# Float64 weights decoded in pieces of 1024 columns into tiles laid out by chunk, with scratch tiles given up one by one

## Chip, cores and metric

The kernel runs on one core of a Trainium2 chip. The metric is the device time of one execution in microseconds (us). Three runs are compared by their median.

## What is computed

Attention over 4 batches and 8 heads, 576 tokens, head size 64, with a mask by blocks of 64; then a gated layer with weights of 512 x 1536; then a layer of 8 experts of which each token takes one.

```python
scores = scale * np.matmul(q, k.transpose(0, 1, 3, 2))
scores = np.where(block_i >= block_j, scores, -1000000000.0)
attn = softmax(scores)                       # written out in the reference
x = np.matmul(attn, v)                       # (4, 8, 576, 64) -> (2304, 512)
gate = 1.0 / (1.0 + np.exp(-(x @ w_gate)))   # w_gate, w_val: 512 x 1536
x = gate * (x @ w_val) @ w_out               # w_out: 1536 x 512
idx = np.argmax(x @ r_gate, axis=1)          # 8 experts
out = prob[idx] * (np.maximum(x @ w1[idx], 0.0) @ w2[idx])
```

`w_gate`, `w_val` and `w_out` reach the kernel as float64, seen as pairs of 32-bit words. The kernel makes of each weight a high and a low float32r part, so that matmuls with both keep float32 accuracy.

## The kernel before

**Stages.** The *quick stage* is attention of batch 0: four pairs of heads (0 to 3), each with five tiles of queries (t = 0 to 4). Then the *gated stage* runs over nine units of 256 tokens (`u`), in each over 12 chunks `f` of 128 columns of the gated layer: `m_gate` and `m_val` (24 matmuls into `gv`), `m_act` (tanh on ScalarE, `th` on VectorE, `g` high on ScalarE, `g` low on VectorE) and, one chunk later, `m_out` (matmuls into `acc`). Attention of batches 1 to 3 is threaded into it. The expert stage ends the kernel. TensorE, VectorE, ScalarE, GpSimd and SyncE are called PE, DVE, ACT, POOL and SP, as in the profile.

**Order.** Every engine runs its instructions in the order in which the program is written. In the quick stage, strings set it: step `i` of `quick` works on tile `a = i + 2` (S scores, M maximum, E exponential, r and c reciprocal of the sum, N scaling), on tile `i + 1` (T, U transposes) and on tile `i` (V product with `v`, X its split into `x`). K and Q transpose the next pair's `k` and `q` and copy them to `kn` and `qn`. A `d` gives the weight decode one step.

```python
Q2 = "SVTMXdUEdrcN"
Q3 = "dSVMXKdTUErcdN"
...
    if i >= 0 and items[i][1] == 0 and 0 < items[i][0]:
        load(items[i][0] + 1)
```

So the loads of the next pair but one (`load`: two heads of `k`, the last tokens of `k` and of `q`, then `q`, then `v`, all on SP's DMA queue) are written at the end of the step with i at t = 0 of a pair; the K that uses them stands in the next step (Q3).

**Decode.** A piece is loaded by one DMA into a ring of raw tiles. On DVE it takes a shift with mask (L545), a mask-and-or (L549), an integer add (L553, shown as CUSTOM or ISA) and the subtraction that gives the low part (L562); on ACT a conversion (L544) and the copy that gives the high part (L560). The raw tile is free after the mask-and-or. The generator `weights` interleaves these steps for three pieces. Chunks 0 to 7 are 24 pieces of 512 columns (`g`, `v`, `o` of each chunk), decoded in scratch cut from six `spare` tiles; a loop drains them all ahead of the gated stage. Then all six spare tiles are given up together, and chunks 8 to 11 follow as 24 pieces of 256 columns in small scratch (`wtmp`, `wt`), during unit 0.

Of the kernel before, what the change touches and what calls it, by code (L numbers as in the profile page):

```python
# [18 lines left out]
P = 128  # L19
# [5 lines left out]
def attn_moe_moe_kernel(  # L25
# [107 lines left out]
    def wtile(name):  # L133
        return wp.tile([P, 2048], F32R, tag="w", name=name, bufs=18)

    FG = KF // 3
    wmat = {}

    spare = [wtile(f"spare{i}") for i in range(6)]

    def wgroup(g):
        for nm in ("g", "v", "o"):
            for part in ("h", "l"):
                wmat[nm, part, g] = wtile(f"w{nm}{part}{g}")

    wgroup(0)
    wgroup(1)

    def w_in(nm, part, kk, f):
        o = kk * 512 + (f % FG) * P  # L150
        return wmat[nm, part, f // FG][:, o:o + P]

    def w_o(part, f):
        o = (f % FG) * 512
        return wmat["o", part, f // FG][:, o:o + 512]


    pairs = [(b, hp) for b in range(B) for hp in range(NP)]
# [241 lines left out]
    def attention():  # L400
# [1 line left out]
        load(0, "kq")  # L402
        wfirst[0](FIRST)
        load(0, "v")
        wfirst[0](4)
        prep(0, "k")
        prep(0, "q")
        load(1)
# [86 lines left out]

    wide = w_gate.dtype == mybir.dt.int64
    wn = 2 if wide else 1
    pieces = []
    upto = []
    for f in range(KF):  # L500
        fo = (f % FG) * P
        n = KD if f < 2 * FG else KD // 2
        for nm, src in (("g", w_gate), ("v", w_val)):
            for a in range(0, KD, n):
                def cut(part, nm=nm, f=f, a=a, n=n, fo=fo):
                    t = wmat[nm, part, f // FG].rearrange("p (k c) -> p k c", k=KD)
                    return t[:, a:a + n, fo:fo + P]
                pieces.append((cut, src, a * P, f * P, n, P))
        for a in range(0, DM, n * P):
            def cut(part, f=f, a=a, n=n):  # L510
                t = wmat["o", part, f // FG].rearrange("p (k c) -> p k c", k=FG)
                return t[:, f % FG:f % FG + 1, a:a + n * P]
            pieces.append((cut, w_out, f * P, a, 1, n * P))
        upto.append(len(pieces))
    wq = []
    wload = [0]
    wdone = [0]
    wlim = [upto[2 * FG - 1]]
    words = spare[0].bitcast(I32).rearrange("p (b c) -> p b c", c=512)
    wb = [words[:, i, :] for i in range(3)]  # L520
    wres = [words[:, 3, :], spare[1].bitcast(I32)[:, 0:512]]
    wring = []

    def w_load(n):
        while wload[0] < min(n, wlim[0]):
            cut, src, r0, c0, nk, ncol = pieces[wload[0]]
            raw_ = wring[wload[0] % len(wring)]
            raw_ = raw_.rearrange("p (k c w) -> p k c w", k=nk, w=wn)
            words = src.bitcast(I32)[r0:r0 + nk * P, c0 * wn:(c0 + ncol) * wn]
            nc.sync.dma_start(  # L530
                out=raw_.rearrange("p k c w -> p k (c w)"), in_=words.rearrange("(k p) c -> p k c", p=P)
            )
            wq.append((cut, raw_))
            wload[0] += 1

    def w_round(n, stage):

        raw_ = wq[n][1]
        nk = raw_.shape[1]
        w0, w1 = raw_[:, :, :, 0], raw_[:, :, :, 1]  # L540
        b = wb[n % len(wb)].rearrange("p (k c) -> p k c", k=nk)
        r = wres[n % 2].rearrange("p (k c) -> p k c", k=nk)
# [12 lines left out]
    def w_split(n, stage):
        cut, raw_ = wq[n]
        nk = raw_.shape[1]
        b = (wb[n % len(wb)].rearrange("p (k c) -> p k c", k=nk) if wide else raw_[:, :, :, 0]).bitcast(F32)
        if stage == 0:
            nc.scalar.copy(out=cut("h"), in_=b)  # L560
        else:
            nc.vector.tensor_tensor(out=cut("l"), in0=b, in1=cut("h"), op=ALU.subtract)  # L562

    def weights(n0):
        n = n0
        while wdone[0] < wlim[0]:
            live = wlim[0]

            def low():
                if n0 <= n - 2 < live:  # L570
                    w_split(n - 2, 1)
                    wdone[0] = n - 1
                    if not wide:
                        w_load(n - 1 + len(wring))

            if len(wb) < 3:
                low()
            if n < live:
                w_load(n + 1)
                if wide:  # L580
                    w_round(n, 0)
            if n0 <= n - 1 < live and wide:
                w_round(n - 1, 2)
                w_load(n - 1 + len(wring))
            if len(wb) == 3:
                low()
            yield
            if n < live and wide:
                w_round(n, 1)
            if n0 <= n - 1 < live:  # L590
                w_split(n - 1, 0)
            n += 1
            yield
# [458 lines left out]
    with tc.manual_schedule():  # L1052
# [9 lines left out]
        wg = [weights(0)]
        for t in spare[2:2 + wn]:
            half = t.bitcast(I32).rearrange("p (b c) -> p b c", c=512 * wn)
            wring.extend(half[:, i, :] for i in range(half.shape[1]))

        pace = [0.0]

        def some(k):
            if done[0] >= -2:  # L1070
                pace[0] += k
                while pace[0] >= 1:
                    pace[0] -= 1
                    next(wg[0], None)

        fill[0] = some
        wfirst[0] = w_load
        while done[0] < NB - 3:
            if done[0] == NB - 4:
                keep = wlim[0]  # L1080
                while wdone[0] < keep:
                    next(wg[0], None)
                del wring[:]
                wgroup(2)
                two = mw.tile([P, 2, 256 * wn], I32, tag="x2t", name="wtmp")
                third = mw.tile([P, 256 * wn], I32, tag="rows", name="wtmp2")
                three = [two[:, 0, :], two[:, 1, :], third]
                wring.extend(three[(x - keep) % 3] for x in range(3))
                wt = ap_.tile([P, 4, 256], I32, name="wt")
                wb[:] = [wt[:, i, :] for i in range(2)]  # L1090
                wres[:] = [wt[:, 2, :], wt[:, 3, :]]
                wlim[0] = len(pieces)
                wg[0] = weights(keep)
                w_load(keep + 3)
# [24 lines left out]
        early = route_early()  # L1119
        for n, (kind, u, f) in enumerate(msegs):  # L1120
            if kind == "g":
                while wdone[0] < upto[f] and u == 0:
                    next(wg[0], None)
                m_gate(u, f)
            elif kind == "v":
                m_val(u, f)
                if f < KF - 1 or not DEFER:
                    m_act(u, f)
                if f == KF - 1 and u + 1 < NU:
                    load_x(u + 1)  # L1130
# [15 lines left out]
            if u == 0:
                pace[0] += max(len(pieces) - wdone[0], 0) / max(PACE * first[1] - n, 2) * 2
                while pace[0] >= 1:
                    pace[0] -= 1
                    next(wg[0], None)  # L1150
# [199 lines left out]
```

## Time and profile before

| what | value |
|---|---|
| median of 3 runs | 1023.14 us (1022.48 to 1024.49) |
| profiled execution, its own time | 1024.85 us |
| its span, first to last instruction | 1023.0 us |
| PE busy | 952.8 us (93%) |
| DVE busy | 627.5 us (61%) |
| ACT busy | 592.9 us (58%) |
| POOL busy | 123.2 us (12%) |
| DMA, mean | 104 GB/s |

The busy shares are means over stages that differ: in the profile's slices of 25.6 us PE is at 6 and 7 tenths in the first four and at 9 nearly throughout later, while DVE is at 9, 9 and 8 tenths in the second to fourth and at 4 to 5 later on. A time that is said to be at some us counts from the start of the span.

### The profile page before, as it was taken

The page shows a single profiled execution, that of the slowest core. Times are in us where ns is not written, and L with a number is a line of the kernel's source. Part 1 is how long each engine was busy: PE and PEld are TensorE (multiplying, and loading weights), DVE is VectorE, ACT ScalarE, POOL GpSimd, SP SyncE. Part 2 cuts the span into 40 slices and gives each one's busy share as a digit, 9 for nine tenths or more (in the row PEclk, how much of TensorE's full clock was granted, in tenths as well). Part 3 has the DMA queues.
Part 4 walks back from the last instruction along what each step waited for, and adds up shares of the span by engine and source line. Part 5 has one row for each costly group of instructions (what it writes and reads, how often), then busy time and mean ns, then how long its engine had stood idle before and what let it go on. Part 6 is the DMA issues. An engine that isn't in the chain of part 4 may idle for free. (4 is left out here: it accounts for less than half of the span.)

```text
span 1023.0 us, 17911 instructions
## 1 busy us (share of the span) xinstructions
PE 952.8 (93%) x6636; PEld 813.3 (80%) x6636; DVE 627.5 (61%) x1262; ACT 592.9 (58%) x1246; POOL 123.2 (12%) x169
## 2 busy tenths in 40 slices
PE   6777988999999999999999999999989999999994
PEld 3444867788888888988888889999968888888883
DVE  5998787645545445545444321122739999888884
ACT  5888556655554554555545321212348888888884
POOL 1111001111101000010000100000012123112110
PEclk9787999999999999999999999999999999999998
DMA  8776341511231131121130110201541552969110
GB/s 224 202 203 192 103 128 59 136 41 44 62 82 38 56 85 38 58 77 46 39 88 14 44 42 1 63 1 63 197 151 65 200 175 97 369 226 334 44 42 19
DMA packets 111514, 106.08 MB, mean 104 GB/s; under 512 B 62271, under 2 KB 83775, under 8 KB 111424
## 3 DMA queue, kind: packets, MB, share of 16 engines
q1 hardware_dynamic: 104480, 84.97, 27.3%
q0 software_dynamic: 6944, 19.93, 5.8%
q8 instruction: 54, 0.88, 0.4%
q14 instruction: 36, 0.29, 0.1%
HBM read 140.53 MB, written 19.40 MB: 156 GB/s over the span
## 5 line engine op out<-in xcount | busy, mean ns | idle before, releaser
L955 DVE TENSOR_TENSOR el<-raw,eh 128x2048 fp32r<-128x2048 f32 x84 | 191.7, 2290 | 26.4 <-ACT eh L954 25.0
L650 PE MATMUL acc<-woh,g 128*128 128x512 f32 x432 | 168.3, 416 | 1.4 <-ACT g L637 1.4
L954 ACT CAST eh<-raw 128x2048 fp32r<-128x2048 f32 x84 | 161.0, 1917 | 2.7 <-DMA raw<-in_moe_w_dram 2.7
L635 DVE SCALAR_TENSOR_TENSOR th<-th,gv 128x256 f32<-128x256 f32 x108 | 45.4, 421 | 152.3 <-ACT th L634 152.2
L613 PE MATMUL gv<-xu,wgh 128*128 128x256 f32 x432 | 128.0, 296 | 0.1
L613 PE MATMUL gv<-xu,wvh 128*128 128x256 f32 x432 | 126.1, 292 | 0.0
L614 PE MATMUL gv<-xu,wgh 128*128 128x256 f32 x432 | 122.4, 283 | 0.0
L615 PE MATMUL gv<-xu,wgl 128*128 128x256 f32 x432 | 122.3, 283 | 0.0
L614 PE MATMUL gv<-xu,wvh 128*128 128x256 f32 x432 | 122.3, 283 | 0.0
L615 PE MATMUL gv<-xu,wvl 128*128 128x256 f32 x432 | 122.3, 283 | 0.0
L634 ACT ACTIVATE th<-gv 128x256 f32<-128x256 f32 x108 | 41.6, 385 | 134.1 <-PE gv L615 133.8
L393 POOL DMA_DIRECT2D x_d<-x x80 | 55.4, 692 | 496.5 <-DVE x L391 291.1
L1001 PE MATMUL hp<-eh,xt 128*128 128x512 f32 x320 | 109.1, 402 | 0.0
L1001 PE MATMUL yp<-eh,ht 128*128 128x512 f32 x320 | 106.1, 393 | 0.7 <-ACT ht L1023 0.7
L650 PEld LDWEIGHTS acc<-woh,g 128*128 128x128 f32 x432 | 81.5, 189 | 18.8 <-issue 3.3
L306 ACT ACTIVATE e<-sp,nm 128x128 f32<-128x128 f32 (+3 forms) x128 | 66.6, 527 | 48.3 <-DVE nm L290 45.1
L613 PEld LDWEIGHTS gv<-xu,wgh 128*128 128x128 f32 x432 | 82.7, 192 | 5.7 <-issue 3.7
L650 PE MATMUL acc<-wol,g 128*128 128x512 f32 x216 | 85.0, 394 | 0.0
L614 PEld LDWEIGHTS gv<-xu,wgh 128*128 128x128 f32 x432 | 82.9, 192 | 1.4
L613 PEld LDWEIGHTS gv<-xu,wvh 128*128 128x128 f32 x432 | 82.9, 192 | 1.2 <-issue 1.2
L614 PEld LDWEIGHTS gv<-xu,wvh 128*128 128x128 f32 x432 | 82.9, 192 | 0.0
L615 PEld LDWEIGHTS gv<-xu,wvl 128*128 128x128 f32 x432 | 82.7, 192 | 0.0
(199 smaller groups left out, 1890.5 us busy)
## 6 DMA issues: line engine op xcount, KB each, us to landing
raw<-in_moe_w_dram SPq DMA_DIRECT2D x88, 1024.0 KB
xu<-x_d SPq DMA_DIRECT2D x36, 256.0 KB
x_d<-x POOLq DMA_DIRECT2D x64, 128.0 KB, 2.6
x_d<-x2r SPq DMA_DIRECT2D x9, 512.0 KB
k<-in_k_dram SPq DMA_DIRECT2D x32, 128.0 KB
q<-in_q_dram SPq DMA_DIRECT2D x32, 128.0 KB
spare<-in_moe_w_gate_dram SPq DMA_DIRECT2D x8, 512.0 KB
v<-in_v_dram SPq DMA_DIRECT2D x32, 128.0 KB
```

What stands on the lines that cost most here:

```text
L306: nc.scalar.activation(out=r["e"][:, j, 0:n], in_=r["view"][:, j, :], func=AF.Exp, bias=r["nm"][:, j:j + 1], accum_out=su[:, j:j + 1],)
L393: nc.gpsimd.dma_start(out=x_d[hp][:, :, t0:t0 + m], in_=x[:, :, 0:m].bitcast(F32))
L613: nc.tensor.matmul(o, lhsT=wh, rhs=x[:, 0, :], start=(kk == 0 and nm == "g"), stop=False, **kw)
L614: nc.tensor.matmul(o, lhsT=wh, rhs=x[:, 1, :], start=False, stop=False, **kw)
L615: nc.tensor.matmul(o, lhsT=wl, rhs=x[:, 0, :], start=False, stop=(kk == KD - 1), **kw)
L634: nc.scalar.activation(out=th, in_=gv[:, 0:UN], func=AF.Tanh, scale=0.5)
L635: nc.vector.scalar_tensor_tensor(out=th, in0=th, scalar=1.0, in1=gv[:, UN:2 * UN], op0=ALU.add, op1=ALU.mult)
L650: nc.tensor.matmul(o, lhsT=g[:, part, hs], rhs=w_o(w, f), start=(f == 0 and w == "h" and part == 0), stop=(f == KF - 1 and part == 1),)
L954: nc.scalar.copy(out=h, in_=raw[j])
L955: nc.vector.tensor_tensor(out=l, in0=raw[j], in1=h, op=ALU.subtract)
L1001: nc.tensor.matmul(o, lhsT=t[:, cs], rhs=w[:, c * 512:(c + 1) * 512], start=(first and c == 0 and part == 0 and w is eh), stop=(last and c ...
```

## The change

The 12 chunks become 18 tiles of 1024 columns high and 1024 low: for each two chunks one tile with `gate` and `val` of the first, one with `out` of both, one with `gate` and `val` of the second. The first 15 are decoded as one piece each, the last three in four pieces of 256 columns. A raw piece of 1024 columns fills a whole spare tile and is loaded by two DMAs; four spare tiles hold raw pieces, one the shifted words, one the converted words. Spare tiles are given up one by one when a later weight tile needs the room. `weights` yields after each step, four times a piece; a `d` counts 0.9 steps. The drain ahead of the gated stage goes; `m_gate` and `m_out` instead each run the generator until the tile of their chunk is done.

```diff
+    FILL = 0.9
...
+    NW = 3 * KF // 2
+    wmat = [wtile(f"w{i}") for i in range(NW - 6)]
+
+    def t_in(f):
+        return 3 * (f // 2) + 2 * (f % 2)
+
+    def t_out(f):
+        return 3 * (f // 2) + 1
...
-        wfirst[0](4)
+        wfirst[0](2)
...
+    NBIG = NW - 3
     pieces = []
...
+    for i in range(NW):
+        f = i // 3 * 2 + (1 if i % 3 == 2 else 0)
+        n = 1024 if i < NBIG else 256
...
+    def count(i):
+
+        return i + 1 if i < NBIG else NBIG + 4 * (i + 1 - NBIG)
...
+    def before(n):
+
+        if n >= NBIG:
+            return three[n % 3], (n - 3 if n >= NBIG + 3 else -1)
+        if n < NW - 6:
+            return words[n % 4], n - 4
+        return words[(n + 1) % 4], n - 3
...
     def w_load(n):
-        while wload[0] < min(n, wlim[0]):
-            cut, src, r0, c0, nk, ncol = pieces[wload[0]]
-            raw_ = wring[wload[0] % len(wring)]
...
+        while wload[0] < min(n, NPI) and before(wload[0])[1] <= wread[0]:
+            dst = before(wload[0])[0]
+            o = 0
+            for src, r0, nk, c0, ncol in pieces[wload[0]][3]:
+                w = nk * ncol * wn
+                x = src.bitcast(I32)[r0:r0 + nk * P, c0 * wn:(c0 + ncol) * wn]
+                nc.sync.dma_start(
+                    out=dst[:, o:o + w].rearrange("p (k c) -> p k c", k=nk), in_=x.rearrange("(k p) c -> p k c", p=P)
+                )
+                o += w
             wload[0] += 1
...
                 out=b, in0=w1, scalar=-0x40000000, in1=b, op0=ALU.bitwise_and, op1=ALU.bitwise_or
             )
+            wread[0] = n
...
+    def weights():
+        n = 0
+        while wdone[0] < NPI:
+            if 0 <= n - 2:
+                w_split(n - 2, 1)
+                yield
+            w_load(NPI)
+            if n < NPI and wide:
+                w_round(n, 0)
+                yield
+            if 0 <= n - 1 < NPI and wide:
                 w_round(n - 1, 2)
...
+                yield
+            if n < NPI and wide:
                 w_round(n, 1)
-            if n0 <= n - 1 < live:
+            w_load(NPI)
+            if 0 <= n - 1 < NPI:
                 w_split(n - 1, 0)
             n += 1
             yield
...
-                keep = wlim[0]
-                while wdone[0] < keep:
-                    next(wg[0], None)
...
             if kind == "g":
-                while wdone[0] < upto[f] and u == 0:
-                    next(wg[0], None)
+                while wdone[0] < count(t_in(f)):
+                    next(wg)
                 m_gate(u, f)
...
             elif kind == "o":
+                while wdone[0] < count(t_out(f)):
+                    next(wg)
                 m_out(u, f, 0)
...
-                pace[0] += max(len(pieces) - wdone[0], 0) / max(PACE * first[1] - n, 2) * 2
+                pace[0] += max(NPI - wdone[0], 0) / max(PACE * first[1] - n, 2) * 4
```

**How it moves instructions.** First, SP's queue where the loads of pair 2 (`k`) stand in the quick stage. Before, the DMA ahead of them is piece 11, of 512 columns:

```order
L530 DMA spare_92<-in_moe_w_val_dram 128x4x256
L530 DMA spare_92<-in_moe_w_out_dram 128x1024
L530 DMA spare_93<-in_moe_w_gate_dram 128x4x256
L186 DMA k<-in_k_dram 128x4x64 x2
L189 DMA k<-in_k_dram 64x2x64
L189 DMA k<-in_q_dram 64x2x64
```

Of the change, the same place; the first five DMAs are the second half of piece 6, piece 7 and piece 8, and piece 8 goes into `spare_90`, which piece 4 had:

```order
L557 DMA spare_92<-in_moe_w_val_dram 128x4x256
L557 DMA spare_93<-in_moe_w_out_dram 128x1024 x2
L557 DMA spare_90<-in_moe_w_gate_dram 128x4x256
L557 DMA spare_90<-in_moe_w_val_dram 128x4x256
L186 DMA k<-in_k_dram 128x4x64 x2
L189 DMA k<-in_k_dram 64x2x64
L189 DMA k<-in_q_dram 64x2x64
```

Ahead of `k` now stand two DMAs of one piece that share one tile, where one DMA stood.

Second, DVE around the reader that these loads wait for. Before, from the mask-and-or of piece 7 (the first row) on; the copy of `k` of pair 2 (`kn<-tp`) comes eight rows behind the last row here:

```order
L549 SCALAR_TENSOR_TENSOR spare_90<-spare_93,spare_90 128x512
L391 TENSOR_TENSOR x<-av,x 128x64
L323 TENSOR_SCALAR su<-su 128x2
L325 RECIPROCAL su<-su 128x2
L545 TENSOR_SCALAR spare_90<-spare_92 128x512
L553 ISA spare_90<-spare_90,spare_91 128x1024
L562 TENSOR_TENSOR wgl_97<-spare_90,wgh_96 128x4x128
L360 TENSOR_SCALAR e<-e,su 128x256 x2
L290 TENSOR_REDUCE nm<-sp 128x2
L391 TENSOR_TENSOR x<-av,x 128x128
L549 SCALAR_TENSOR_TENSOR spare_90<-spare_92,spare_90 128x512
L545 TENSOR_SCALAR spare_90<-spare_92 128x512
```

Of the change, the mask-and-or of piece 4 (third row) and what follows up to that copy:

```order
L391 TENSOR_TENSOR x<-av,x 128x128
L579 ISA spare_94<-spare_94,spare_95 128x2048
L574 SCALAR_TENSOR_TENSOR spare_94<-spare_90,spare_94 128x1024
L323 TENSOR_SCALAR su<-su 128x2
L325 RECIPROCAL su<-su 128x2
L290 TENSOR_REDUCE nm<-sp 128x2
L391 TENSOR_TENSOR x<-av,x 128x128
L223 COPY kn<-tp 128x576
```

The reader for which the last weight load ahead of `k` waits has moved from nineteen rows ahead of the copy to five.

Third, DVE where the gated stage begins (`ka` and `ql` are the next batch's `k` and `q`, `th` and `g` belong to chunk 0). Before:

```order
L234 TENSOR_TENSOR ka<-tp,ka 64x576
L235 TENSOR_TENSOR ka<-tp,ka 64x576
L237 SCALAR_TENSOR_TENSOR ql<-tp,qa 64x64 x2
L545 TENSOR_SCALAR wt<-wtmp 128x256
L553 ISA wt<-wt 128x512
L325 RECIPROCAL su<-su 128x1
L366 TENSOR_SCALAR e<-e,su 128x576
L237 SCALAR_TENSOR_TENSOR ql<-tp,qa 64x512 x2
L549 SCALAR_TENSOR_TENSOR wt<-wtmp,wt 128x256
L635 SCALAR_TENSOR_TENSOR th<-th,gv 128x256
L638 TENSOR_TENSOR g<-th,g 128x256
```

Of the change:

```order
L234 TENSOR_TENSOR ka<-tp,ka 64x576
L235 TENSOR_TENSOR ka<-tp,ka 64x576
L237 SCALAR_TENSOR_TENSOR ql<-tp,qa 64x64 x2
L570 TENSOR_SCALAR spare_94<-spare_91 128x1024
L325 RECIPROCAL su<-su 128x1
L366 TENSOR_SCALAR e<-e,su 128x576
L237 SCALAR_TENSOR_TENSOR ql<-tp,qa 64x512 x2
L579 ISA spare_94<-spare_94,spare_95 128x2048
L574 SCALAR_TENSOR_TENSOR spare_94<-spare_91,spare_94 128x1024
L656 SCALAR_TENSOR_TENSOR th<-th,gv 128x256
L659 TENSOR_TENSOR g<-th,g 128x256
```

The same three decode steps stand ahead of `th`, with 1024 columns for 256.

## Rows read from the trace of the kernel before

**Rows 1.** Windows of the quick stage, of 101 to 200 us and of 200 to 700.

```profile
core 0: us, PE busy (x) PEld busy (x) DVE busy (x) ACT busy (x) POOL busy (x), PEclk, DMA share, GB/s
20.00:101.00 81.00, 59.57 (x421) 37.23 (x418) 76.38 (x177) 66.84 (x176) 12.91 (x22) 0.81 0.71 203
101.00:200.00 99.00, 86.88 (x663) 75.94 (x663) 72.46 (x207) 59.55 (x173) 9.82 (x19) 0.98 0.39 111
200.00:700.00 500.00, 490.75 (x3882) 438.03 (x3877) 209.21 (x567) 224.90 (x635) 40.47 (x77) 1.00 0.18 49
```

**Rows 2.** Groups of instructions on DVE up to 101 us, by shape.

```profile
line engine op names shapes xcount | busy us, mean ns | idle before us <-releasers
L549 DVE SCALAR_TENSOR_TENSOR spare<-spare,spare 128x512 int32<-128x512 int32 x24 | 16.3, 677 | 0.0
L545 DVE TENSOR_SCALAR spare<-spare 128x512 int32<-128x512 int32 x24 | 11.5, 480 | 0.0
...
L562 DVE TENSOR_TENSOR wol<-spare,woh 128x512 fp32r<-128x512 f32 x8 | 5.5, 683 | 0.1
...
L290 DVE TENSOR_REDUCE nm<-sp 128x2 f32<-128x1024 f32 x4 | 4.9, 1217 | 0.0
```

**Rows 3.** Timeline of DVE, a piece of 512 and one of 256 columns.

```profile
start us, us, engine line op out<-in xcount [idle before <-releaser]
92.35 0.42 DVE L545 TENSOR_SCALAR spare<-spare 128x512 int32<-128x512 int32 x1
92.69 0.68 DVE L553 CUSTOM_DVE_ANT_0 spare<-spare 128x1024 uint16<-128x1024 uint16 x1
93.29 0.69 DVE L562 TENSOR_TENSOR wgl<-spare,wgh 128x512 fp32r<-128x512 f32 x1
93.89 0.16 DVE L323 TENSOR_SCALAR su<-su 128x2 f32<-128x2 f32 x1
...
113.55 0.29 DVE L545 TENSOR_SCALAR wt<-wtmp 128x256 int32<-128x256 int32 x1
113.76 0.42 DVE L553 CUSTOM_DVE_ANT_0 wt<-wt 128x512 uint16<-128x512 uint16 x1
114.09 0.42 DVE L549 SCALAR_TENSOR_TENSOR wt<-wtmp,wt 128x256 int32<-128x256 int32 x1
```

**Rows 4.** Timeline of SP's queue, the loads of piece 11 and pair 2.

```profile
38.35 0.34 SPq L530 DMA_DIRECT2D spare<-in_moe_w_out_dram  x1
38.74 0.99 SPq L186 DMA_DIRECT2D k<-in_k_dram  x2
```

**Rows 5.** Timelines of DVE and PE, from that load's release to its use.

```profile
37.59 0.68 DVE L549 SCALAR_TENSOR_TENSOR spare<-spare,spare 128x512 int32<-128x512 int32 x1
...
44.95 0.48 PE L216 MATMUL tp<-ident,k 128*128 128x128 f32 x1
...
45.47 1.22 DVE L290 TENSOR_REDUCE nm<-sp 128x2 f32<-128x1024 f32 x1
...
47.09 0.75 DVE L223 COPY kn<-tp 128x576 f32<-128x576 f32 x1
...
49.66 0.17 DVE L323 TENSOR_SCALAR su<-su 128x2 f32<-128x2 f32 x1
```

**Rows 6.** Timelines of SP's queue and PE, the first load of `k`.

```profile
0.76 0.99 SPq L186 DMA_DIRECT2D k<-in_k_dram  x2
...
4.00 1.51 PE L216 MATMUL tp<-ident,k 128*128 128x128 f32 x5 [4.00 <-DMA k<-in_k_dram]
```

**Rows 7.** Windows of 1 us with weights, then `q` and `v`, on the way.

```profile
34.00:35.00 1.00, 1.00 (x8) 0.27 (x6) 0.97 (x5) 1.00 (x4) 0.43 (x1) 0.50 1.05 372
43.00:44.00 1.00, 1.00 (x6) 0.24 (x6) 1.00 (x3) 1.00 (x5) 0.84 (x2) 0.50 1.17 218
```

**Rows 8.** Timelines of DVE and PE, gated stage of unit 0.

```profile
103.63 0.75 DVE L234 TENSOR_TENSOR ka<-tp,ka 64x576 fp32r<-64x576 f32 x1 [1.97 <-ACT qa L230]
...
108.79 0.42 DVE L635 SCALAR_TENSOR_TENSOR th<-th,gv 128x256 f32<-128x256 f32 x1
...
109.70 0.50 PE L650 MATMUL acc<-woh,g 128*128 128x512 f32 x1 [1.44 <-ACT g L637]
...
140.08 0.33 PE L337 MATMUL ep<-ident,e 128*128 128x128 f32 x1 [3.46 <-ACT et L339]
```

More of the change, by code (lines that the diff above doesn't have):

```diff
@@ L134, in wtile @@
         return wp.tile([P, 2048], F32R, tag="w", name=name, bufs=18)
-    FG = KF // 3
-    wmat = {}
     spare = [wtile(f"spare{i}") for i in range(6)]
[L141 to L147, printed above, removed]
+    NW = 3 * KF // 2
[4 more added lines that the diff above has]
+        return 3 * (f // 2) + 1
     def w_in(nm, part, kk, f):
-        o = kk * 512 + (f % FG) * P
-        return wmat[nm, part, f // FG][:, o:o + P]
+        o = (1024 if part == "l" else 0) + (512 if nm == "v" else 0) + kk * P
+        return wmat[t_in(f)][:, o:o + P]
     def w_o(part, f):
-        o = (f % FG) * 512
-        return wmat["o", part, f // FG][:, o:o + 512]
+        o = (1024 if part == "l" else 0) + (f % 2) * 512
+        return wmat[t_out(f)][:, o:o + 512]
     pairs = [(b, hp) for b in range(B) for hp in range(NP)]
@@ L497, in attn_moe_moe_kernel @@
     wn = 2 if wide else 1
+    NBIG = NW - 3
     pieces = []
[L499 to L514, printed above, removed]
@@ L515, in attn_moe_moe_kernel @@
-    wq = []
+    for i in range(NW):
+        f = i // 3 * 2 + (1 if i % 3 == 2 else 0)
+        n = 1024 if i < NBIG else 256
+        for c in range(0, 1024, n):
+            ld = []
+            if i % 3 == 1:
+                m = min(n, 512)
+                for o in range(c, c + n, 512):
+                    ld.append((w_out, (f + o // 512) * P, 1, o % 512, m))
+            else:
+                m = min(n, 512) // P
+                for o in range(c, c + n, 512):
+                    ld.append((w_gate if o < 512 else w_val, o % 512, m, f * P, P))
+            pieces.append((i, c, n, ld))
@@ L516, in attn_moe_moe_kernel @@
+    NPI = len(pieces)
+    def count(i):
+        return i + 1 if i < NBIG else NBIG + 4 * (i + 1 - NBIG)
     wload = [0]
     wdone = [0]
[L518 to L522, printed above, removed]
-    def w_load(n):
-        while wload[0] < min(n, wlim[0]):
-            cut, src, r0, c0, nk, ncol = pieces[wload[0]]
-            raw_ = wring[wload[0] % len(wring)]
[L528 to L533, printed above, removed]
+    wread = [-1]
@@ new lines, in attn_moe_moe_kernel, with w_raw @@
+    words = [t.bitcast(I32) for t in spare]
+    two = mw.tile([P, 2, 256 * wn], I32, tag="x2t", name="wtmp")
+    third = mw.tile([P, 256 * wn], I32, tag="rows", name="wtmp2")
+    three = [two[:, 0, :], two[:, 1, :], third]
+    wt = ap_.tile([P, 4, 256], I32, name="wt")
+    def before(n):
[4 more added lines that the diff above has]
+        return words[(n + 1) % 4], n - 3
+    def w_raw(n):
+        w = pieces[n][2]
+        return before(n)[0][:, 0:w * wn].rearrange("p (c w) -> p c w", w=wn)
@@ new lines, in w_buf, with w_res @@
+    def w_buf(n):
+        if not wide:
+            return w_raw(n)[:, :, 0]
+        return words[4][:, (n % 2) * 1024:(n % 2 + 1) * 1024] if n < NBIG else wt[:, n % 2, :]
+    def w_res(n):
+        return words[5][:, (n % 2) * 1024:(n % 2 + 1) * 1024] if n < NBIG else wt[:, 2 + n % 2, :]
+    def w_load(n):
+        while wload[0] < min(n, NPI) and before(wload[0])[1] <= wread[0]:
[8 more added lines that the diff above has]
+                o += w
@@ L534, in w_load @@
             wload[0] += 1
     def w_round(n, stage):
[L538 to L542, printed above, removed]
+        raw_ = w_raw(n)
+        w0, w1 = raw_[:, :, 0], raw_[:, :, 1]
+        b, r = w_buf(n), w_res(n)
         if stage == 0:
@@ L555, in w_split @@
     def w_split(n, stage):
-        cut, raw_ = wq[n]
-        nk = raw_.shape[1]
-        b = (wb[n % len(wb)].rearrange("p (k c) -> p k c", k=nk) if wide else raw_[:, :, :, 0]).bitcast(F32)
+        i, c, w, _ = pieces[n]
+        while len(wmat) <= i:
+            wmat.append(wtile(f"w{len(wmat)}"))
+        b = w_buf(n).bitcast(F32)
+        h, l = wmat[i][:, c:c + w], wmat[i][:, 1024 + c:1024 + c + w]
         if stage == 0:
-            nc.scalar.copy(out=cut("h"), in_=b)
+            nc.scalar.copy(out=h, in_=b)
         else:
[L562 to L582, printed above, removed]
-                w_round(n - 1, 2)
[L584 to L588, printed above, removed]
+            nc.vector.tensor_tensor(out=l, in0=b, in1=h, op=ALU.subtract)
+            wdone[0] = n + 1
+            if not wide:
+                wread[0] = n
+    def weights():
[9 more added lines that the diff above has]
+            if 0 <= n - 1 < NPI and wide:
+                w_round(n - 1, 2)
+                yield
+            if n < NPI and wide:
                 w_round(n, 1)
-            if n0 <= n - 1 < live:
+            w_load(NPI)
+            if 0 <= n - 1 < NPI:
                 w_split(n - 1, 0)
@@ L1060, in seg @@
             return r is not None
[L1062 to L1065, printed above, removed]
+        wg = weights()
         pace = [0.0]
@@ L1070, in some @@
             if done[0] >= -2:
-                pace[0] += k
+                pace[0] += k * FILL
                 while pace[0] >= 1:
                     pace[0] -= 1
-                    next(wg[0], None)
+                    next(wg, None)
         fill[0] = some
@@ L1079, in attn_moe_moe_kernel @@
             if done[0] == NB - 4:
-                keep = wlim[0]
-                while wdone[0] < keep:
-                    next(wg[0], None)
[L1083 to L1094, printed above, removed]
                 load_x(0)
@@ L1121, in attn_moe_moe_kernel @@
             if kind == "g":
-                while wdone[0] < upto[f] and u == 0:
-                    next(wg[0], None)
+                while wdone[0] < count(t_in(f)):
+                    next(wg)
                 m_gate(u, f)
@@ L1146, in attn_moe_moe_kernel @@
             if u == 0:
-                pace[0] += max(len(pieces) - wdone[0], 0) / max(PACE * first[1] - n, 2) * 2
+                pace[0] += max(NPI - wdone[0], 0) / max(PACE * first[1] - n, 2) * 4
                 while pace[0] >= 1:
                     pace[0] -= 1
-                    next(wg[0], None)
+                    next(wg, None)
             if extra and f < KF - 1 and (kind == "p" or u == NU - 1):
```

## Prediction

> **What bounds the kernel now.** The windows view comes first [rows 1]. From 20 to 101 us VectorE (DVE) is busy 76.38 of 81 us; PE has 59.57, ScalarE (ACT) 66.84, and PE's granted clock is 0.81. That is the quick stage, attention of batch 0 with the weight decode threaded through it. From 101 to 200 us PE is busy 86.88 of 99, from 200 to 700 us 490.75 of 500. So time saved on DVE before 101 us brings the whole rest forward one for one; later, only what opens or closes a hole in PE counts. 12.1 us of PE holes lie between 101 and 200 us.
>
> Next the groups of the decode [rows 2]: of 24 pieces of 512 columns, the masked shift takes 480 ns, the mask-and-or 677 ns; the add and the subtraction are as long as the latter. Durations overlap their successors, so starts are the price that counts. In [rows 3] shift, add and subtraction of 512 columns begin 0.34, 0.60 and 0.60 us before the next instruction; at 256 columns a shift begins 0.21 and an add 0.33 us before it. A piece of 512 thus costs DVE 0.34 + 3 x 0.60 = 2.14 us.
>
> **Decode in the quick stage: -7 us.** The order of DVE shows, ahead of the first `ka` subtraction, 24 whole pieces plus the first two steps of a small one before, and 12 first, 12 second, 11 third and 11 fourth steps of 1024 columns now. By starts a shift of 1024 is 0.34 + 2 x 0.13 = 0.60 us, each other step 0.60 + 2 x 0.27 = 1.14 us. Before: 24 x 2.14 + 0.54 = 51.9 us. Now: 12 x 1.74 + 11 x 2.28 = 46.0 us; 5.9 us less, 2.3 us of it merely because piece 11's last two steps move behind the stage. The other bound takes whole durations: a reduction over 1024 columns takes 1217 ns [rows 2], a shift about 0.74, so 24 x (0.48 + 3 x 0.68) + 0.7 = 61.2 us against 12 x 1.96 + 11 x 2.44 = 50.4 us, 10.8 us less. I take 7, near the starts, since [rows 3] show them back to back; the extra 1 is for fewer waits between the steps of a piece.
>
> [...]
>
> **Weight loads ahead of `k`: +9.5 us.** A raw piece is now 1 MB in two DMAs, and the load of piece n+4 stands in SP's queue right behind the mask-and-or of piece n, the last reader of its tile. The order of SP shows that `k` of pair 2 comes behind piece 8's load, hence behind mask-and-or 4. On DVE that stands five rows ahead of the copy `kn<-tp` of that same `k`; between them are two `su` rows, a reduction and `x`. Before, the load ahead of `k` (piece 11) waits for mask-and-or 7, nineteen rows ahead of the copy: it ends at 37.59 + 0.68 = 38.27, the load goes out at 38.35 and `k` at 38.74 [rows 4], PE transposes it at 44.95 and DVE copies it at 47.09 [rows 5]. That slack of 6.2 us is what goes.
>
> Let T be the end of mask-and-or 4. Two `su` rows of 0.16 us and the reduction follow, so in the distances of [rows 5] (reduction 45.47, copy 47.09, next `su` 49.66) the copy is due at T+1.9 and PE wants `k` at about T-0.2. The load goes out at T+0.1, `k` two issues later at T+0.9. The first `k` of the kernel goes out at 0.76 and PE takes it at 4.00 [rows 6], 3.2 us later with nothing ahead. Bound below: `k` passes the weights and is there at T+4.1. Bound above: it follows them. 1 MB at 372 GB/s takes 2.8 us and 256 KB of `k` at 218 GB/s 1.2 us [rows 7]; with 2.0 us from issue to first data (3.2 less 1.2) that is T + 0.1 + 2.0 + 2.8 + 1.2 = T+6.1. The copy comes 0.95 us of transposes (five times, [rows 5] has the first) and a short ACT copy later, about 1.15 us: T+5.2 to T+7.2, so 3.3 to 5.3 us late. Pair 3 is built alike: `k` behind piece 11, behind mask-and-or 7, with one subtraction of 1.14 us more in between, so 2.2 to 4.2 us late. DVE runs in order, so the attention and decode steps behind the copy wait too, and ACT's exponentials and PE's transposes behind the late `k`. Sum 5.5 to 9.5; as `su` hangs on ACT's chain, which starts later still than the copy, up to 11. I take 9.5, the case in which one queue serves in order. `v` and `q` of these pairs, behind `k` too, are needed a step later and have cover; `k` of pair 4 has two steps and is free.
>
> [...] No run so far shows `k` behind a load of this size.
>
> **Start of the gated stage: +1.5 us.** Before, DVE starts `ka` at 103.63, `th` of chunk 0 at 108.79, and PE waits 1.44 us for `g` until 109.70 [rows 8]. The order shows the same shift, add and mask-and-or ahead of that `th`, now of 1024 columns: 0.39 + 0.81 + 0.81 = +2.0 us on a chain that PE already waits for. Then, between `th` of chunk 0 and of chunk 2, stand nine long steps instead of twelve small ones (7 x 1.14 + 2 x 0.60 = 9.2 against 9 x 0.33 + 3 x 0.21 = 3.6 us). 5.6 us more on DVE; PE's work there hides most and 1 to 2.4 us shows at chunks 2 and 3. After them 11 small pieces are left against 16, some 5 x 1.2 us less in front of the holes that the attention chain leaves, like the 3.46 us at 140.08 [rows 8]. I give back 3 of the 12.1 us of holes. 2.0 + 2.4 - 3 = 1.5; bounds -2 and +4.5.
>
> **At nothing.** Dropping the forced drain before the gated stage: three subtractions and an add, counted above. New chunk layout and per-chunk waits: PE's matmuls and GpSimd's instructions stand in the same order with the same shapes, and tile 11, the first that PE could wait for (chunk 7), is subtracted at chunk 0. ACT's share of the decode shrinks in the same way, but at 66.84 us of 81 it is not the bound.
>
> **Sum.** -7 + 9.5 + 1.5 = +4.0. The profiled execution took 1024.85 us (span 1023.0); it would become 1028.9. The median of the runs is 1023.14, so 1027.1; I say 1027.
>
> **Rivals.**
> (a) Faster: `k` comes in time. If DMAs overlap more than in order, or DVE runs behind PE by more than [rows 5] show, the copy is not held: -7 + 1.5 = -5.5, 1017.6 us. For it: `k` before lands with room. Against: even the uncontended 3.2 us of the first `k` pass T+1.9. It decides when the two stalls together cost under 3.5 us. By whole durations it would be -9.3, 1013.8.
> (b) No change: the stalls at their lower bound and an even gated stage: -7 + 5.5 + 0.5 = -1, 1022 us.
> (c) Much slower: nothing comes back from the holes and the stalls stand at 10.5: -7 + 10.5 + 4.5 = +8, 1031 us.
> A DVE no longer the bound (ACT or the chain takes over, saving halved) ends near (c) too: +7.5.
>
> **Numbers.** Forecast 0.38, (a) 0.27, (b) 0.2, (c) 0.15. 0.2% of the time is 2 us, about what a measurement of this kernel can tell from no change. Faster 0.27, same 0.2, slower 0.53. The range leaves a tenth outside on either side: 1016, into (a), to 1032, past (c). The forecast's own is 1025 to 1030.
>
> **What would show it.** In the new trace: one idle of 3 us or more on DVE at `kn<-tp` of pair 2 and of pair 3, with PE waiting for DMA `k` just ahead; shifts of 1024 near 0.7 us and other steps near 1.22; PE's wait for `g` of chunk 0 near 3.4 us; smaller holes after chunk 4. No wait of PE for `k` would make (a) right; DVE idle all through the quick stage would make the saving wrong.

## The result, and the profile after

The changed kernel takes 1032.67 us (median of 4 runs, 1031.55 to 1036.45) against 1022.81 beside it: ratio 1.010, 95% interval 1.0071 to 1.0130. Run once more later it took 1034.54 against 1023.73, ratio 1.0104 (1.0080 to 1.0128). It is slower, by 9.9 and 10.8 us. The forecast was +4 and 1027; the range ended at 1032.

The windows view of the changed kernel, as in [rows 1]:

```profile
20.00:101.00 81.00, 48.73 (x373) 30.40 (x373) 62.55 (x117) 55.56 (x137) 11.44 (x21) 0.83 0.61 185
101.00:200.00 99.00, 82.22 (x612) 70.52 (x614) 72.74 (x173) 59.92 (x156) 9.68 (x19) 0.98 0.41 115
200.00:700.00 500.00, 490.56 (x3900) 438.10 (x3900) 211.93 (x574) 228.09 (x644) 41.16 (x78) 1.00 0.18 50
```

In the quick stage all engines are busy for less time: DVE 62.55 us against 76.38, PE 48.73 against 59.57. Less work alone would lower DVE's figure; that PE, which has no part in the decode, falls with it means that they stand still together. From 200 to 700 us the figures are alike. Two marks make this exact. From DVE's first `kn` copy to its first `ka` subtraction it is 81.0 us before (22.62 to 103.63) and 89.3 after (21.86 to 111.14; 90.4 in the second execution). From `ka` to the end of unit 0 (the start of ACT's first `x2r` row) it is 86.1 before and 87.8 after (89.3 in the second execution).

The waits of DVE from `kn` to `ka`: for what, us in sum, how often, the longest. First the kernel before:

```profile
DVE su L323 <- ACT e L306: 2.3, 5, 0.8
DVE ka L234 <- ACT qa L230: 2.0, 1, 2.0
DVE x L391 <- ACT x L390: 1.3, 6, 0.3
```

Then the changed kernel:

```profile
DVE kn L223 <- ACT qn L221: 11.8, 2, 6.2
DVE su L323 <- ACT e L306: 5.6, 7, 1.8
DVE x L391 <- ACT x L390: 2.0, 4, 0.8
DVE ka L234 <- ACT qa L230: 1.4, 1, 1.4
DVE su L323 <- ACT e L315: 0.2, 1, 0.2
```

Take the sums, 5.6 and 21.0 us, from the lengths: DVE's own work falls from 75.4 to 68.3 us, by 7.1, and its waits grow by 15.4. 11.8 of that is the copy of a late `k`. The chain can be read across three timelines of the changed kernel. DVE, with the mask-and-or that the load waits for, and the copy of `kn`:

```profile
40.18 1.22 DVE L574 SCALAR_TENSOR_TENSOR spare<-spare,spare 128x1024 int32<-128x1024 int32 x1
41.32 0.16 DVE L323 TENSOR_SCALAR su<-su 128x2 f32<-128x2 f32 x1
...
43.07 0.29 DVE L391 TENSOR_TENSOR x<-av,x 128x128 fp32r<-128x128 f32 x1 [0.28 <-ACT x L390]
49.57 0.76 DVE L223 COPY kn<-tp 128x576 f32<-128x576 f32 x1 [6.21 <-ACT qn L221]
50.24 1.22 DVE L590 TENSOR_TENSOR w<-spare,w 128x1024 fp32r<-128x1024 f32 x1
52.45 0.17 DVE L323 TENSOR_SCALAR su<-su 128x2 f32<-128x2 f32 x1 [1.00 <-ACT e L306]
...
69.34 1.22 DVE L574 SCALAR_TENSOR_TENSOR spare<-spare,spare 128x1024 int32<-128x1024 int32 x1
...
78.88 0.76 DVE L223 COPY kn<-tp 128x576 f32<-128x576 f32 x1 [5.59 <-ACT qn L221]
```

SP's queue, which answers to [rows 4]:

```profile
41.46 0.38 SPq L557 DMA_DIRECT2D spare<-in_moe_w_gate_dram  x1
41.88 0.51 SPq L557 DMA_DIRECT2D spare<-in_moe_w_val_dram  x1
42.49 1.00 SPq L186 DMA_DIRECT2D k<-in_k_dram  x2
```

PE, which answers to [rows 5]:

```profile
47.98 1.30 PE L216 MATMUL tp<-ident,k 128*128 128x128 f32 x5 [7.78 <-DMA k<-in_k_dram]
...
77.28 1.30 PE L216 MATMUL tp<-ident,k 128*128 128x128 f32 x5 [6.71 <-DMA k<-in_k_dram]
```

T, the end of the mask-and-or, is 40.18 + 1.22 = 41.40. The weights go out at T+0.1, `k` at T+1.1, PE has it at T+6.6, DVE copies at T+8.2. DVE was ready at 49.57 - 6.21 = 43.36, T+2.0. The row of DVE names ACT, which makes a copy of 0.23 us first (`qn`, at 49.31); PE's row names the DMA. Pair 3 repeats it: T = 69.34 + 1.22 = 70.56, PE at T+6.7, the copy at T+8.3. PE's wait covers 40.2 to 48.0 us, DVE's 43.4 to 49.6: one late load holds both.

The decode by shape on DVE up to 112 us, to set beside [rows 2]:

```profile
L574 DVE SCALAR_TENSOR_TENSOR spare<-spare,spare 128x1024 int32<-128x1024 int32 x12 | 14.5, 1212 | 0.0
L590 DVE TENSOR_TENSOR w<-spare,w 128x1024 fp32r<-128x1024 f32 x11 | 13.4, 1217 | 0.0
L579 DVE CUSTOM_DVE_ANT_0 spare<-spare,spare 128x2048 uint16<-128x2048 uint16 x11 | 13.3, 1212 | 0.0
L570 DVE TENSOR_SCALAR spare<-spare 128x1024 int32<-128x1024 int32 x12 | 8.3, 688 | 0.0
```

The start of the gated stage, DVE and then PE, to set beside [rows 8]:

```profile
111.14 0.75 DVE L234 TENSOR_TENSOR ka<-tp,ka 64x576 fp32r<-64x576 f32 x1 [1.36 <-ACT qa L230]
...
118.66 0.42 DVE L656 SCALAR_TENSOR_TENSOR th<-th,gv 128x256 f32<-128x256 f32 x1 [0.39 <-ACT th L655]
```

```profile
112.75 0.39 PE L634 MATMUL gv<-xu,w 128*128 128x256 f32 x1 [1.51 <-DMA xu<-x_d]
114.60 0.58 PE L634 MATMUL gv<-xu,w 128*128 128x256 f32 x1 [1.23 <-DMA xu<-x_d]
...
137.20 1.64 PE L671 MATMUL acc<-w,g 128*128 128x512 f32 x6 [0.96 <-ACT g L658]
```

The first `th` comes 7.5 us after `ka` (5.2 before), but PE waits there for `xu`, the input of the gated stage, not for `g`. `xu` is late for the same reason as `k`. It stands behind the loads of pair 4 in SP's queue, and these behind a weight load that waits for a mask-and-or (98.19 to 99.41 on DVE). The changed kernel, then the kernel before:

```profile
99.47 0.84 SPq L557 DMA_DIRECT2D spare<-in_moe_w_out_dram  x2
100.41 0.93 SPq L186 DMA_DIRECT2D k<-in_k_dram  x2
...
106.26 2.53 SPq L623 DMA_DIRECT2D xu<-x_d  x4
```

```profile
89.43 10.04 SPq L602 DMA_DIRECT2D xu<-x_d  x4
```

Before, the first `xu` goes out 14.2 us ahead of `ka`, now 4.9 us. Near the end of unit 0 PE has one more wait that the kernel before does not have, for the low part of a weight tile (for what, us in sum, how often, the longest):

```profile
PE gv L636 <- DVE w L590: 1.6, 1, 1.6
```

### The profile page after: what moved, and what is told of

It is laid out like the page before. It is cut to its first block, busy times and chain, and to the rows that moved or that the text cites. A ratio compares the mean times of both kernels' runs of the same rounds, so it can differ in the third digit from the quotient of the medians.

```text
span 1029.8 us, 17756 instructions
## 1 busy us (share of the span) xinstructions
PE 945.8 (92%) x6636; PEld 808.7 (79%) x6636; DVE 618.5 (60%) x1178; ACT 588.7 (57%) x1204; POOL 124.8 (12%) x169
## 5 line engine op out<-in xcount | busy, mean ns | idle before, releaser
L634 PE MATMUL gv<-xu,w 128*128 128x256 f32 x864 | 254.1, 294 | 3.0 <-DMA xu<-x_d 3.0
L636 PE MATMUL gv<-xu,w 128*128 128x256 f32 x864 | 244.5, 283 | 1.6 <-DVE w L590 1.6
L635 PE MATMUL gv<-xu,w 128*128 128x256 f32 x864 | 244.5, 283 | 0.0
L671 PE MATMUL acc<-w,g 128*128 128x512 f32 x648 | 183.3, 409 | 1.1 <-ACT g L658 1.0
L634 PEld LDWEIGHTS gv<-xu,w 128*128 128x128 f32 x864 | 165.3, 191 | 10.6 <-issue 5.0
L635 PEld LDWEIGHTS gv<-xu,w 128*128 128x128 f32 x864 | 165.6, 192 | 1.4
L636 PEld LDWEIGHTS gv<-xu,w 128*128 128x128 f32 x864 | 165.2, 191 | 1.8 <-DVE w L590 1.8
L671 PEld LDWEIGHTS acc<-w,g 128*128 128x128 f32 x648 | 110.9, 189 | 21.4 <-issue 3.3
L658 ACT CAST g<-th 128x256 fp32r<-128x256 f32 x108 | 43.9, 406 | 67.0 <-DVE th L656 62.4
L659 DVE TENSOR_TENSOR g<-th,g 128x256 fp32r<-128x256 f32 x108 | 45.9, 425 | 53.4 <-ACT g L658 53.4
L382 PE MATMUL av<-et,v 128*64 128x128 f32 (+1 forms) x960 | 65.8, 268 | 8.0 <-ACT et L339 7.8
L337 PE MATMUL ep<-ident,e 128*128 128x128 f32 x320 | 58.1, 288 | 13.8 <-DVE e L360 5.6
L1022 PEld LDWEIGHTS yp<-eh,ht 128*128 128x128 f32 x320 | 59.9, 188 | 13.7 <-ACT ht L1044 0.9
L1022 PEld LDWEIGHTS hp<-eh,xt 128*128 128x128 f32 x320 | 60.2, 188 | 11.8
```

Source lines behind the costliest of these rows:

```text
L337: nc.tensor.transpose(ep[:, cs], r["e"][:, part, cs], ident)
L382: nc.tensor.matmul(av[hs, 0:m], lhsT=d["v"][:, c, j, :], rhs=rhs, start=(c == 0), stop=(c == t))
L634: nc.tensor.matmul(o, lhsT=wh, rhs=x[:, 0, :], start=(kk == 0 and nm == "g"), stop=False, **kw)
L635: nc.tensor.matmul(o, lhsT=wh, rhs=x[:, 1, :], start=False, stop=False, **kw)
L636: nc.tensor.matmul(o, lhsT=wl, rhs=x[:, 0, :], start=False, stop=(kk == KD - 1), **kw)
L659: nc.vector.tensor_tensor(out=g[:, 1, :], in0=th, in1=g[:, 0, :], op=ALU.subtract)
```

## Experiments

Theory 1: the slowdown is the late `k` of pairs 2 and 3, and without it the change saves time. Theory 1a adds that it is late for two reasons, the wait of the load ahead of it for a mask-and-or, and that load's megabyte. Rivals: the slowdown sits in the gated stage, or in the coarser steps themselves. "Length" is from the first `kn` to `ka`; "unit 0" is the end of unit 0. Each ratio is to the kernel before, timed beside it.

**The changed kernel again.** 

> The changed kernel as it is, once more, for the scatter of the marks that the other runs are compared by. If these are sound, DVE starts the copies of k at 21.9, 49.6 and 78.9 us, the first subtraction of ka at 111.1 and ACT the end of unit 0 at 199.0, each within 0.7 us, and the median is 1031 to 1034 us. If the idle times of 6.21 and 5.59 us were luck of one execution, the marks move by 2 us or more.

Length 90.4, idle at `kn` 6.21 and 5.61, `ka` 112.85, unit 0 at 202.2. The stalls repeat to 0.02 us; `ka` moves by 1.7, unit 0 by 3.2, both more than the 0.7 I had allowed. So one execution tells a mark in the gated stage to some 3 us only (the last section shows what goes with it).

**Loads of `k`, `q`, `v` at the start of their step.** The edit in the loop of quick steps, ahead of the letters that issue weight loads:

```diff
+            if i >= 0 and items[i][1] == 0 and 0 < items[i][0]:
+                load(items[i][0] + 1)
             for c in QUICK[t].split()[0]:
...
-            if i >= 0 and items[i][1] == 0 and 0 < items[i][0]:
-                load(items[i][0] + 1)
```

In the changed kernel: 

> The changed kernel with one edit: the loads of the next pair but one are written at the start of their step, ahead of the weight load that waits for a mask-and-or, instead of at its end. Order on DVE, ACT and PE is as in the changed kernel. Theory 1 (k of pairs 2 and 3 is held behind the weight load): both waits of PE for DMA k vanish, the idle of 6.2 and 5.6 us on DVE at kn goes, with the 1.0 and 1.8 us at the next su; 14 us less than the changed kernel, so 1017 to 1020 us. Rival 2 (DVE and PE lose the time anyway, since larger pieces leave the attention chain waiting): the idle moves to other instructions, and the time stays within 4 us of the changed kernel's 1032.7.

Again: 

> The changed kernel with the loads of k first, once more. Work of DVE from the first copy of k to ka 68.3 us and idle time there 8.0 us again, each within 0.3; the end of unit 0 near 189.4 us within 3; median 1021 to 1024. If the waits of 8.0 us were luck of one execution, they move by 1 us or more.

Measured 1022.62 (ratio 0.9984, 0.9967 to 1.0002) and 1021.79 (0.9980, 0.9960 to 1.0000). PE and DVE in the second execution:

```profile
42.02 0.78 PE L216 MATMUL tp<-ident,k 128*128 128x128 f32 x5
```

```profile
44.02 0.75 DVE L223 COPY kn<-tp 128x576 f32<-128x576 f32 x1
44.68 1.22 DVE L590 TENSOR_TENSOR w<-spare,w 128x1024 fp32r<-128x1024 f32 x1
46.13 0.17 DVE L323 TENSOR_SCALAR su<-su 128x2 f32<-128x2 f32 x1 [0.23 <-ACT e L306]
```

No idle at `kn`; length 76.2 and 77.4. The stalls thus cost 89.85 - 76.8 = 13.0 us of length (means of two). Theory 1 holds; both medians are above the 1020 that I had as its upper end, by 2.6 and 1.8 us. In the second execution PE no longer waits for `xu` either: the page of the changed kernel has 3.0 us of idle for it, this one none. Waits of the second execution, `kn` to `ka`:

```profile
DVE su L323 <- ACT e L306: 4.2, 8, 1.0
DVE x L391 <- ACT x L390: 3.1, 5, 1.0
DVE ka L234 <- ACT qa L230: 1.4, 1, 1.4
DVE su L323 <- ACT e L315: 0.2, 1, 0.2
```

8.9 us (8.1 in the first execution), where before had 5.6: these 2.5 to 3.3 us of the saving go to waits for ACT without any stall.

**The same edit in the kernel before.** 

> The kernel before with the same edit alone. Theory 1: k already landed in time there, so within 1 us of before. Rival 3 (the early k load is worth something by itself, through PE or the DMA engines): 2 us or more faster.

1025.62, ratio 1.0008 (0.9992 to 1.0024), `ka` 103.74 against 103.63. There `k` was in time, as [rows 4, 5] said, so the order of loads by itself is worth nothing that this run shows.

**Only 16 KB of the two pieces ahead of `k`, the rest behind `v`.** The core of the edit:

```diff
+            if wload[0] in (8, 11):
+                src, r0, nk, c0, ncol = pieces[wload[0]][3][0]
+                nc.sync.dma_start(out=dst[:, 0:32], in_=src.bitcast(I32)[r0:r0 + P, c0 * wn:c0 * wn + 32])
+                held.append((wload[0], dst))
+                wload[0] += 1
+                continue
```

> The changed kernel, but of pieces 8 and 11 only the first 32 words of each row (16 KB) are loaded ahead of k, waiting for the same mask-and-or; the whole piece follows behind v. So k still waits for the mask-and-or, but has no 1 MB ahead of it. Theory 1a (queue in order, the megabyte costs its transfer): the idle at kn falls from 6.2 and 5.6 us to about 3.3 and 2.5, 6 to 7 us less in total. Rival 1b (the wait for the mask-and-or and the fixed time of a DMA make up the stall, the data ahead of k does not matter): the idle stays above 5 us each, the total within 2 us of the changed kernel.

```profile
47.77 0.76 DVE L223 COPY kn<-tp 128x576 f32<-128x576 f32 x1 [3.73 <-ACT qn L221]
...
74.12 0.76 DVE L223 COPY kn<-tp 128x576 f32<-128x576 f32 x1 [2.51 <-ACT qn L221]
```

1031.25, ratio 1.0073 (1.0046 to 1.0099). `k` stands behind the same mask-and-or, but not behind the data. Of 11.8 us of idle, 6.2 stay: they are the wait and the load's own latency; the other 5.6 (2.5 and 3.1) are the megabyte with its second DMA. Without them `k` of pair 2 goes out at T+0.5 instead of T+1.1, and from there to PE it takes 3.3 us instead of 5.5; the first `k` of the kernel, with nothing ahead, took 3.2 [rows 6]. The length is 84.3, 5.5 us less. Theory 1a holds for the idle and the length. The time hardly tells: the interval overlaps that of the changed kernel, and 1031.25 is 1.4 and 3.3 us below its two medians; the gated stage of the profiled execution took 89.4 us, as long as in the second one of the changed kernel.

**Less decode in the quick stage:** `FILL = 0.85` for 0.9, which also puts 14 or 15 rows between mask-and-or and copy. 

> The changed kernel with one number edited: FILL 0.85 instead of 0.9, the k loads at the end of their step as there. The mask-and-or that the weight load ahead of k waits for then stands 15 and 14 rows ahead of the copies of pairs 2 and 3, not 5 and 6. Theory 1 (what costs is where that reader happens to stand): the idle at both copies falls under 1.5 us, the first ka comes at 99 to 101.5 us of the span instead of 111.1, and the time is 8 to 12 us under the changed kernel. Rival 4 (any load of 1 MB ahead of k in one queue costs this much): the idle stays at 4 us or more for each pair.

1026.97, ratio 1.0028 (1.0014 to 1.0043): 5.7 us under the changed kernel's 1032.67, not 8 to 12. Idle at `kn` falls to 0 and 0.61, so rival 4 falls and the place of the reader counts, but `ka` comes at 103.12, not at 99 to 101.5. The waits:

```profile
DVE su L323 <- ACT e L306: 9.3, 13, 1.6
DVE x L391 <- ACT x L390: 2.4, 7, 0.7
```

DVE works some 1.7 us less than with 0.9 and waits 4 to 5 us more for ACT than with the loads first. Less decode made the stage longer (length 80.5 us here and 80.3 with the loads first too, below, against 76.2 and 77.4), so the waits grow by more than the work that is gone, and the number of steps alone does not explain them. That it is where the steps stand among the attention steps is the reading that is left; no run moves the steps alone.

**Gated pace by columns,** beside loads first, alone, and with FILL 0.85. The loop that hands out decode steps in unit 0 counted pieces, a large one like a small one:

```diff
-                pace[0] += max(NPI - wdone[0], 0) / max(PACE * first[1] - n, 2) * 4
+                left = sum(x[2] for x in pieces[wdone[0]:]) / 256
+                pace[0] += left / max(PACE * first[1] - n, 2) * 4
                 while pace[0] >= 1:
-                    pace[0] -= 1
+                    pace[0] -= pieces[min(wdone[0] + 1, NPI - 1)][2] / 256
```

Beside loads first: 

> As e1, and in the gated stage the decode is paced by columns left instead of pieces left, so that large pieces are spread wider. If the crowding of large pieces behind th of chunks 0 to 3 costs the time that the start of the gated stage lost (2.4 us up to the first th, 1 to 2.4 us at chunks 2 and 3): 1 to 3 us less than e1. Rival: what is lost there comes back later in unit 0 either way, and e3 is within 1 us of e1.

Again: 

> The same with the even pace. If the even pace is worth something once the quick stage ends early, the end of unit 0 lies 3 to 5 us before that of the kernel with k first alone and the median 1.5 to 4 us below its. The rival, from the run in which pace alone brought nothing: both end within 1.5 us of each other, and the difference between 1022.62 and 1020.85 was scatter.

Alone: 

> The changed kernel with the gated stage's pace counted in columns alone, its loads of k left where they are. If the two costs are separate, the quick stage stays (ka near 111.1) and the end of unit 0 comes some 4 us sooner than in the changed kernel (199.0 to about 195), median about 1028. The rival: in the changed kernel the gated stage already gave back 4.8 us after chunk 3 because ACT's chain, not decode, set its end; then an even pace brings under 1.5 us there.

With FILL 0.85: 

> Loads of k first, even pace, and FILL 0.85: less decode in the quick stage, more in the gated one. If decode costs DVE more in the quick stage than in the gated one (FILL 1.0 cost 6.2 us), ka comes 3 to 5 us before the 99.48 of the kernel with FILL 0.9 and the end of unit 0 0 to 3 us before its 185.3: 1018 to 1021 us. If the waits that grew in the run with FILL 0.85 alone come from where the steps stand among the attention steps, ka stands within 1.5 us of 99.5 or later and the end of unit 0 is 1 to 5 us later.

The first gave 1020.85, ratio 0.9972 (0.9954 to 0.9991), with unit 0 at 185.3, four us before the kernel with loads first. That did not last. Side by side the two gave 1021.67 (0.9970, 0.9957 to 0.9983) and 1021.79, unit 0 at 188.0 and 187.6; alone the pace gave 1037.98 (1.0135, 1.0112 to 1.0159), 3.4 us above the changed kernel beside it, with `ka` at 112.57 and unit 0 at 203.2, not near 195. The gain was scatter, as the rivals had it: the pace is worth nothing that shows. Alone it looks worse still, but the intervals overlap. With 0.85 it is 1027.17, ratio 1.0027 (1.0013 to 1.0041), DVE's waits for `e` 9.4 us, `ka` 102.16: the second theory of that run again, and unit 0 at 194.5, 9.2 us later, more than the 5 it allowed.

**More decode in the quick stage,** the same with `FILL = 1.0`. 

> As e3 with FILL 1.0: more of the decode lies in the quick stage. DVE bounds that stage, so ka comes 4 to 6 us later than e3's 99.5 (one and a third pieces of 4 us); the gated stage has that much less. If decode is cheaper beside matmuls: unit 0 ends 1 to 3 us after e3's 185.3. If the gated stage is as short of DVE as the quick stage: within 1 us of it.

1025.58, ratio 1.0011 (0.9995 to 1.0026); `ka` 104.97, 5.5 us later as said, DVE's work 72.7 us and 2.0 of idle at `kn`. But unit 0 ends at 191.5, 6.2 and 3.5 us after the two executions with 0.9 (185.3 and 188.0), where both theories had at most 3. Most of what moved into the quick stage is not given back in the gated one.

**The drain put back,** beside loads first and even pace: all twelve large pieces finished ahead of the gated stage.

```diff
+                while wdone[0] < 12:
+                    next(wg)
```

> As e3 (k first, even pace), with the drain put back: the first 12 tiles are decoded ahead of the gated stage. The prediction priced dropping the drain at nothing beside the moved steps. If so: ka comes later by the moved work (about 2 to 3 us), and the end of unit 0 within 1.5 us of e3's 185.3. Rival: waiting for tiles one by one is worth 2 us or more, so that unit 0 ends after 187.3.

1021.49, ratio 0.9973 (0.9961 to 0.9986). `ka` is 5.0 us later, more than the 2 to 3 I had said, and unit 0 (186.3) lies between the two executions without the drain (185.3 and 188.0). Beside loads first, dropping the drain is worth about nothing, as forecast; in the changed kernel itself it was not tried.

**No decode from the last quick step to the first `th`:** `if -2 <= done[0] < NB - 4` in the quick stage's filler, `if u == 0 and n >= 2` in the gated one's. 

> As e3, with no decode step between the last quick step and th of chunk 0. Theory (decode ahead of the first th delays PE one for one): the first th comes 4 to 5 us after ka instead of 6.0 and 7.5, and unit 0 ends 1 to 2 us before e3's 185.3. Rival (it comes back in the holes later): within 1 us of e3.

1025.46, ratio 1.0014 (0.9998 to 1.0031). `th` comes 4.2 us after `ka` as meant, but unit 0 ends at 190.0. PE from 101 to 200 us:

```profile
PE ep L337 <- ACT et L339: 4.4, 1, 4.4
PE gv L634 <- ACT w L588: 2.4, 1, 2.4
```

PE waits later for a decoded tile (2.4 us, for `w`): the wait moved. This theory fell. (This execution spent 17.1 us from `ka` to the end of unit 0 at a granted clock of 0.50, the two with the even pace 3.4 and 10.2, so part of the difference is the clock's.)

## Why the forecast was right in direction and too small

**Bound: right.** What shifted before `ka` shifted the end. From the end of unit 0 to the end of the span it is 833.3 us before and 830.8 and 831.4 in the changed kernel; over all the runs here it is 830.2 to 836.0.

**Decode -7: work right, net wrong.** DVE's own work fell by 7.1 us, where the starts had given 5.9; steps are 1.21 to 1.22 and shifts 0.69 us long, as written. The decode's own subtraction of 1024 columns took 1217 ns, as long as the reduction that the bound by whole durations had set in its place. The 10.8 us of that bound did not come, as consecutive instructions overlap: the mask-and-or at 40.18 lasts 1.22 us, the next row starts 1.14 us after it. But two steps failed: "the extra 1 is for fewer waits", and ACT set at nothing because it "is not the bound". Without stalls DVE waits 2.5 to 3.3 us more for ACT. The net saving is 81.0 - 76.8 = 4.2 us. That is most of the way to the aside in the rivals, a DVE no longer the sole bound with the saving halved. Why these waits grow stays open.

**Weight loads ahead of `k`, +9.5: right mechanism, mis-sized term.** It measured 13.0. `k` came at T+6.6 and T+6.7, not T+6.1. The copy stood 1.6 us behind the transposes' start, not 1.15: after its wait PE ran the five in 1.30 us at a granted clock of 0.50, against 0.78 us at 1.00 with the loads first, where it had not waited. Idle at `kn` was 6.21 and 5.59 where the upper bounds were 5.3 and 4.2: 2.3 us more. The rest, 13.0 - 11.8 = 1.2, is mostly the `su` behind (in pair 2 1.00 against 0.23 us), which the text named and left out of the 9.5. The lower bounds, 3.3 and 2.2, are close to the 3.73 and 2.51 of the run in which `k` has 16 KB ahead of it. That `k` follows the weights and does not pass them, the case behind the 9.5, was the author's estimate. The runs bear it out for this load: from its issue to PE `k` took 5.5 and 5.6 us behind the data; without that and its second DMA, in pair 2, it took 3.3 us and reached PE at T+3.8, 2.8 us sooner, and in pair 3 DVE copied at T+5.2, 3.1 us sooner. The windows with the transposes of pair 2, changed kernel and loads first (PE's clock is the third number from the end):

```profile
47.00:50.00 3.00, 2.02 (x10) 2.05 (x11) 0.43 (x1) 0.27 (x2) 0.00 (x0) 0.50 1.23 233
```

```profile
42.00:43.00 1.00, 0.81 (x7) 0.56 (x5) 0.96 (x4) 0.57 (x2) 0.00 (x0) 1.00 1.33 264
```

**Gated stage +1.5: size right within the scatter, path not.** It measured +1.7 in the first execution (86.1 to 87.8) and +3.2 in the second. PE's wait of 3.4 us for `g` did not show, since `xu` was late first: two waits, 2.7 us. The step that missed them is "`k` of pair 4 has two steps and is free": that `k` was in time, but `xu` stood behind it in the queue. With `k` first `xu` is in time, `th` again comes 7.5 us after `ka`, and PE waits for `g` up to 3.1 us, so the chain was sized well. The hole of 3.46 us in [rows 8] shrank to 1.4, as said. "At nothing" was wrong for the waits of PE for single tiles: the text looked as far as tile 11, but in chunk 11 PE waits 1.6 us for the last tile's decode.

**The sum** becomes -4.2 + 13.0 + 1.7 = +10.5, or +12.0 with the second execution's gated stage, against 9.9 and 10.8 measured. Rival (a) needed `k` in time, and fell. (c), 1031, was nearest, though its reason was another. The range took its upper end from stalls of 10.5 with the full saving of 7; both were off in one direction. So the forecast missed by two terms: the stalls were taken 3.5 us too small and the saving 2.8 us too large, since the waits grew where they were to shrink.

## What to carry to other kernels

When transfers are merged, look at what stands behind the larger one in its queue: here a load that waited for a buffer held the loads behind it, needed or not (`k` twice, with 11.8 us of idle on DVE, and `xu` once, with 2.7 us of waits on PE), and its bytes came on top, with 5.6 of the 11.8 us. Put the loads that the next step needs ahead of those that only refill. Here that turned a loss of 10 us into a time 0.2% under the kernel before, which neither of its two runs alone puts clear of no change; with the even pace too it is 0.3%, and both intervals end below 1. And price a saving on the busiest engine with the waits that it uncovers: here 7.1 us less work on DVE were worth 4.2, as its waits for ACT grew by 2.5 to 3.3 us.

## What the runs showed of the hardware

PE's granted clock goes with the scatter in the gated stage. The same changed kernel had it at the lower level (0.50) for 3.4 us in sum there in one execution and for 10.2 in the other, counted in windows of 1 us. PE's busy time from `ka` to the end of unit 0 was 74.51 and 77.55 us, while its idle time, 13.4 and 11.75, did not grow. First execution, then second:

```profile
111.10:199.00 87.90, 74.51 (x558) 65.09 (x557) 65.46 (x160) 49.36 (x135) 6.89 (x13) 0.98 0.34 98
```

```profile
112.90:202.20 89.30, 77.55 (x559) 67.93 (x559) 65.38 (x160) 49.26 (x134) 6.91 (x13) 0.94 0.34 96
```

The two other kernels that were run twice agree: loads first spent 10.3 and 3.4 us at the lower level and took 90.9 and 87.8 us from `ka` to the end of unit 0, and with the even pace too it was 3.4 and 10.2, and 85.8 and 88.6 us. In the first execution the low stretch begins at 114 us, behind PE's two waits for `xu` (1.51 and 1.23 us); the kernel before had none there (its own comes at 141 us, behind the 3.46 us wait). So the clock hides what the even pace does: with loads first it cut PE's idle time in this stretch from 13.8 and 14.3 us to 11.4 and 11.9, but its second execution spent 10.2 us at 0.50 against 3.4 in the kernel that it was timed beside, and the end came no sooner. The clock stayed at 1.00 behind the 1.44 us wait for `g` in the kernel before, and behind waits of 1.88 and 2.04 us in the first execution of the changed kernel (PE's rows at 159.65 and 179.60); why stays open.
